# V of three token groups by wide products and SBUF-to-SBUF placing, with the zero fill, the w1 loads and the engine order rewritten around it

## The chip, the cores and the metric

The kernel runs on one core of a Trainium2 chip. TensorE multiplies matrices, VectorE (DVE in the profile) and GpSimd (POOL) work elementwise, ScalarE (ACT) evaluates functions, and SyncE (SP) issues nearly all transfers here. The metric is the device time in microseconds of one execution; four runs before the change have a median of 273.91 us (272.58 to 274.77).

## The reference

One block of a model: attention in a sliding window, then a token mixer, both with modulation by a condition vector `c`. S = 2048 tokens, D = 512, 32 heads of width 16, window 256, F = 1792.

```python
mod = (silu(c) @ w_mod).reshape(1, 6, 1, -1)          # sa, ca, ga, sb, cb, gb
h = layernorm(x) * (1 + ca) + sa
q, k, v = heads(h @ wqkv)
p = softmax(where(0 <= i - j < 256, q @ k.T / 4, -1e9))
x = x + ga * ((p @ v) @ wo)
h = layernorm(layernorm(x) * (1 + cb) + sb)
u = gelu(einsum('bsd,sf->bdf', h, w1) + b1)            # mixes tokens
x = x + gb * (einsum('bdf,fs->bds', u, w2) + b2).T
```

## The kernel before

**Stages.** The tokens are cut into four groups G of 512. For each group `proj` (line 518) normalizes x, transposes it to `h1T`, and forms Q, K and V; `attention` (line 854) is called for two units of 256 queries, and `post` (line 713) applies `wo`, adds the residual and makes the mixer's input `hb`. `partials` (line 787) and the loops at the end do the mixer's two large products: `pu<-hb,w1p` and `pu<-guT,w`.

**Attention.** It goes in 75 chunks. A chunk has scores for four heads at a time (`S`, TensorE, into `psa` and `psb`), two exponentials on ScalarE (`E` of 128x1536 and `F` of 128x512, into a ring of six `et` tiles), masks, and the product with V (`AV`, into `pxy`). In units 0 to 3 the masking is done on TensorE, by adding products of `edge_w` with `edge_n` or `edge_t`; in later units VectorE multiplies `et` by `maskt`. A unit's sums are normalized by `ln`, `rz` (ScalarE, tile `lz`) and `OT` (VectorE). Chunks 0 to 14 belong to group 0, 15 to 34 to group 1, 35 to 54 to group 2, 55 to 74 to group 3.

**V.** Keys go in blocks of 64. An AV product of a head pair has 128 rows: 64 keys of even heads above, 64 of odd heads below, and 32 weight columns, 16 for each parity; the half of V's columns that belongs to the other parity has to be zero. `VT` (line 244) is a ring of three such tiles, each filled with zeros once by `vt_zero` (line 512), all three on GpSimd. `v` (line 659) handles one block of 128 tokens: 32 matmuls of 128x32 weights with 256 columns put even heads into the upper partitions of `pv` and odd heads into the lower ones, so that two evacuations of 64 partitions each write straight to their places in `VT`. With four blocks in each of four groups there are 16 such blocks.

**K.** `k` (line 621) evacuates to `kb`, from which GpSimd (`kk`) writes two masked copies into `KT`.

**Order.** Every piece of work is an `Op` with dependencies. `ORDER` (line 42) is an order written out by hand number by number, with a letter where an operation isn't on its first engine; `run_order` (line 101) emits by it, and the emitted order is each engine's program order. The costs and positions in the `op` calls take no part in that. SP's queue also follows it: a transfer that waits holds up the ones behind it.

**w1.** `partials` frees the modulation weights' memory and then issues seven loads of 512 KB (`w1p`), which in the written order come together around chunk 18. A second half of each follows when the first has been used. The first product with w1 comes after chunk 46.

All instructions of the main part carry line 193, the wrapper that records order, so the profile is read by tile names.

## Time and profile before

| | |
|---|---|
| median of four runs | 273.91 us (272.58 to 274.77) |
| profiled execution: its time, its span | 273.24 us, 271.4 us |
| mean granted TensorE clock | 0.990 |
| TensorE busy | 250.9 us (92%) |
| VectorE busy | 209.0 us (77%) |
| ScalarE busy | 184.8 us (68%) |
| GpSimd busy | 68.3 us (25%) |
| HBM read, written | 22.03 MB, 2.10 MB |
| VT evacuations | 31 on VectorE, 686 ns each; 1 on ScalarE, 590 ns |
| VT zero fills on GpSimd | 3 of 3.51 us |

A group line of the profile names the engine and operation, written tile <- read tiles, the shape, the count, then busy time and mean duration in ns, then the idle time of the engine just before these instructions and what ended it. "issue" means that nothing shown was waited for. Busy time of TensorE counts pipelined matmuls by their modelled ends. In the timeline a line starts with start and length in us.

### The profile page before, as it was taken

What the parts mean: (1) busy time and instruction counts of PE and PEld (TensorE: products, weight loads), DVE (VectorE), ACT (ScalarE), POOL (GpSimd) and SP (SyncE); (2) the same over time, 40 slices, a digit from 0 to 9 for tenths busy, and PEclk for the clock granted to TensorE, in tenths of its full rate; (3) what the DMA queues carried; (4) which work ended last, traced back from release to release, by engine and by line L of the source; (5) the groups of instructions that cost most, each with busy time, mean ns of one, the idle gap of its engine ahead of it and who ended that gap; (6) DMA issues with size and microseconds to landing.
All of it is one profiled execution on the core that took longest, in us unless ns stands there. A gap on an engine that the chain in (4) does not pass through costs nothing.

```text
span 271.4 us, 10569 instructions
## 1 busy us (share of the span) xinstructions
PE 250.9 (92%) x4737; PEld 137.9 (51%) x4737; DVE 209.0 (77%) x442; ACT 184.8 (68%) x277; POOL 68.3 (25%) x131
## 2 busy tenths in 40 slices
PE   8879979699998999777999999999999999999993
PEld 2556647256766664445464454445544444444441
DVE  4788899578987678999977799999999751134685
ACT  3369969589998999999999999999632741000000
POOL 8994460135021844152102410140000000000000
PEclk9999999799999999999999999999999999999998
DMA  6998104940000000000020000095199800011121
GB/s 208 324 350 208 5 2 133 290 129 5 2 5 5 2 6 2 2 2 2 12 74 2 2 2 4 2 238 153 52 392 384 334 2 4 19 39 39 62 90 65
DMA packets 31445, 24.80 MB, mean 91 GB/s; under 512 B 6056, under 2 KB 29608, under 8 KB 31400
## 3 DMA queue, kind: packets, MB, share of 16 engines
q1 hardware_dynamic: 31392, 24.13, 29.4%
q8 instruction: 37, 0.61, 1.0%
q14 instruction: 8, 0.07, 0.1%
q10 hardware_dynamic: 8, 0.00, 0.0%
HBM read 22.03 MB, written 2.10 MB: 89 GB/s over the span
## 4 chain that ended last, share of the span: by engine, by line
PE 73%; ACT 11%; DVE 10%; issue 4%
PE pu L193 35%; PE pxy L193 13%; ACT et L193 10%; PE pq L193 8%; PE psa L193 8%; PE pa L193 4%; PE pv L193 3%; DVE st L193 2%; DVE VT L193 1%; DVE xn L193 1%; ACT lz L193 1%; PE pt L193 1%; DVE nm L193 1%; DVE et L193 1%; PE ps_b L193 1%
## 5 line engine op out<-in xcount | busy, mean ns | idle before, releaser
L193 ACT ACTIVATE et<-psa 128x1536 bf16<-128x1536 f32 x75 | 109.0, 1454 | 9.9 <-PE psb L193 7.2
L193 PE MATMUL pu<-hb,w1p 128*128 128x512 bf16 x224 | 53.0, 380 | 0.1
L193 PE MATMUL pu<-guT,w 128*128 128x512 bf16 x224 | 49.2, 379 | 0.0
L193 ACT ACTIVATE et<-psb 128x512 bf16<-128x512 f32 x75 | 44.6, 598 | 0.0
L193 POOL TENSOR_SCALAR KT<-kb,mask_par 128x512 bf16<-128x512 bf16 (+1 forms) x36 | 23.2, 652 | 63.1 <-DVE kb L193 63.1
L193 PE MATMUL pxy<-et,VT 128*32 128x192 bf16 (+3 forms) x960 | 37.5, 234 | 0.7 <-DVE OT L193 0.5
L193 PE MATMUL pxy<-et,ones_bd 128*32 128x192 bf16 (+3 forms) x960 | 37.6, 233 | 0.2 <-issue 0.2
L193 PE MATMUL pq<-h1T,wqkv 128*128 128x512 bf16 (+1 forms) x160 | 35.3, 347 | 2.6 <-DVE kb L193 1.5
L193 PEld LDWEIGHTS <-w 128*128 128x128 bf16 x224 | 21.9, 98 | 26.4
L193 PE MATMUL psa<-QT,KT 32*128 32x192 bf16 (+3 forms) x720 | 30.0, 230 | 5.1 <-ACT et L193 4.2
L193 PEld LDWEIGHTS <-w1p 128*128 128x128 bf16 x224 | 20.2, 98 | 24.9 <-issue 1.9
L193 PE MATMUL psb<-QT,KT 32*128 32x192 bf16 (+3 forms) x240 | 29.5, 231 | 2.7 <-issue 2.5
L193 PEld LDWEIGHTS <-KT 32*128 32x128 bf16 x960 | 15.6, 92 | 28.8 <-issue 27.2
L193 DVE SCALAR_TENSOR_TENSOR o<-pu,b2FM,bc_gb 128x512 f32<-128x512 f32 x16 | 12.0, 748 | 23.1 <-PE pu L193 23.0
L193 PEld LDWEIGHTS <-VT 128*32 128x32 bf16 x960 | 23.6, 97 | 7.7 <-issue 6.2
L193 DVE TENSOR_TENSOR et<-et,maskt 128x512 bf16<-128x512 bf16 (+2 forms) x56 | 23.8, 459 | 1.5 <-ACT et L193 1.4
L193 PEld LDWEIGHTS <-ones_bd 128*32 128x32 bf16 x960 | 23.2, 97 | 0.4 <-issue 0.3
L193 DVE CAST VT<-pv 64x512 bf16<-64x512 f32 x31 | 21.1, 686 | 2.9 <-PE pv L193 2.6
L193 DVE BATCH_NORM_STATS2 st<-x 128x6 f32<-128x512 bf16 x32 | 21.9, 683 | 1.9 <-DMA x<-in_A_x_dram 1.8
L193 PEld LDWEIGHTS <-wqkv 128*128 128x128 bf16 x160 | 13.4, 99 | 14.9 <-issue 5.4
L193 PE MATMUL pv<-wqkv,h1T 128*32 128x256 bf16 x512 | 17.8, 274 | 0.7 <-DVE h1T L193 0.6
L193 DVE CAST QT<-pq 128x512 bf16<-128x512 f32 (+1 forms) x19 | 13.1, 687 | 5.6 <-PE pq L193 5.5
(91 smaller groups left out, 347.4 us busy)
## 6 DMA issues: line engine op xcount, KB each, us to landing
w1p<-in_B_w_dram SPq DMA_DIRECT2D x14, 512.0 KB, 7.4
w<-in_B_w_dram SPq DMA_DIRECT2D x14, 512.0 KB, 8.9
wmod<-in_w_mod_dram SPq DMA_DIRECT2D x6, 512.0 KB, 6.6
x<-in_A_x_dram SPq DMA_DIRECT2D x16, 128.0 KB, 5.7
out_dram<-otile SPq DMA_DIRECT2D x16, 128.0 KB, 1.7
wqkv<-in_A_wqkv_dram SPq DMA_DIRECT2D x2, 384.0 KB, 6.1
wqkv<-in_A_wqkv_dram SPq DMA_DIRECT2D x1, 512.0 KB, 5.8
wod<-in_A_wo_dram SPq DMA_DIRECT2D x1, 512.0 KB, 9.5
```

What stands on the lines that cost most here:

```text
L193: ins = call(*args, **kwargs)
```

## The change

`v` now handles groups 1 to 3 only; group 0 keeps the old form as `v_first`. The new `v` takes 128 tokens as weights and all 512 V columns as moving data: four matmuls of 128x512. One evacuation writes the tile `vn`, parity by parity, with two buffers. Then four transfers of 64 partitions by 512 bytes, issued by SP, copy each parity's part of each 64-key block to its rows in `VT`. `VT` is laid out with the 16 heads of a parity innermost, so an AV weight tile reads 32 columns at a step of 16 elements; both evacuations therefore read PSUM at a step.

Around it: each zero fill is cut into four, of which five of twelve are put on VectorE and seven on GpSimd. The negated mean `nm`, where VectorE makes it, is computed as -2m + m by an operation of two tensors. Edges and masks are two operations; scores of units 0 to 3 wait for the edges, later masks for the masks. Each first-half w1 load waits for a `touch`, a two-element GpSimd copy from `et` of chunk 17, 20, ... 35, and the written order issues these loads one at a time between chunks 31 and 55. The order is new throughout; among the 1414 operations some change engine (for instance three Q evacuations on ScalarE instead of one, 13 normalizations `n2` on VectorE instead of 10).

```diff
@@ -43,58 +43,60 @@
 ORDER = """
-47 3 0 4 34 1 51 2 38 7 35 8 39 5 82 56 40 81 6 46 9 57 54 83 10 45 11 49 58 12 84 48 13 43 14 59 37 15 60 16 52 61
-85D 17 63 90D 18 55 91D 19 64 20 94 53 21 96D 97 44 95D 22 99A 50 86 78P 41 23 98A 106 36 24 109 25 107 42 26 108D
...
+45 3 0 4 41 78D 1 50 55 2 32 7 40 8 48 5 93 56 34 80P 6 37 9 57 52 10 58 90 42 11 46 12 79D 35 13 94 39 14 47 15 59
+95 96D 16 60 31 61 17 101D 63 18 62 102D 19 51 20 64 105 21 108 106A 33 22 110D 36 107A 38 109D 23 43 97 117 24 120
+121 25 118 122D 53 26 119A 49 123D 27 132 85D 28 133 140 29 134D 84P 141 196 98 30 142A 135 197 136 151 137D 152
...
 """
@@ -114,6 +116,7 @@
 E_BUFS = 6
+VN_BUFS = 2
 WARM = 24
@@ -241,7 +244,7 @@
     KT = [[kvpool.tile([P, 8, 2, KB], BF, name=f"KT{r}_{g}") for g in range(ND)] for r in range(3)]
-    VT = [kvpool.tile([P, 8, DH, 2 * DH], BF, name=f"VT{r}") for r in range(3)]
+    VT = [kvpool.tile([P, 8, 2 * DH, DH], BF, name=f"VT{r}") for r in range(3)]
     epool = att.enter_context(tc.tile_pool(name="epool", bufs=E_BUFS))
@@ -288,10 +291,6 @@
     def emit_masks():
-        if ADDED:
-            emit_edges()
-        if len(ADDED) == NU:
-            return
         tmpm = modw.tile([P, 2, 2, KB], BF, name="tmpm")
@@ -465,8 +464,12 @@
             mv, _, nm = box[box_key]
-            (ve if e == "DVE" else po).tensor_scalar(
-                out=nm[:, a:b], in0=mv[:, a:b, 0], scalar1=-1.0, scalar2=0.0, op0=ALU.mult, op1=ALU.add)
+            if e == "DVE":
+                ve.scalar_tensor_tensor(
+                    out=nm[:, a:b], in0=mv[:, a:b, 0], scalar=-2.0, in1=mv[:, a:b, 0], op0=ALU.mult, op1=ALU.add)
+            else:
+                po.tensor_scalar(
+                    out=nm[:, a:b], in0=mv[:, a:b, 0], scalar1=-1.0, scalar2=0.0, op0=ALU.mult, op1=ALU.add)
@@ -492,7 +495,7 @@
                     if pool:
-                        both.append(op(f"{tag}nm", {"DVE": 0.1, "POOL": 0.2}, lambda e, a=a, b=b: e_nm(e, a, b), deps=st_ops[:], pos=poss[i]))
+                        both.append(op(f"{tag}nm", {"DVE": 0.16, "POOL": 0.2}, lambda e, a=a, b=b: e_nm(e, a, b), deps=st_ops[:], pos=poss[i]))
                     for k in range(a, b):
@@ -509,8 +512,9 @@
-    vt_zero = [op("vz", {"DVE": 1.7, "POOL": 4.3}, lambda e, r=r: (ve if e == "DVE" else po).memset(VT[r][:], 0.0), pos=-20.0 + 5 * r)
-               for r in range(3)]
+    v_placed = []
+    vt_zero = [[op("vz", {"DVE": 0.45, "POOL": 0.95}, lambda e, r=r, n=n: (ve if e == "DVE" else po).memset(VT[r][:, 2 * n : 2 * n + 2, :, :], 0.0),
+                   pos=-20.0 + 5 * r, sh=True) for n in range(4)] for r in range(3)]
     k_done, q_done, v_done = {}, {}, {}
@@ -649,7 +653,7 @@
                 done = [
-                    op("kk", {"POOL": 0.1 + 0.6 * share}, lambda e, par=par: split(e, box["kb", g8], par), deps=[b, o_mp] + war, pos=pos, sh=True)
+                    op("kk", {"POOL": 0.1 + 0.66 * share}, lambda e, par=par: split(e, box["kb", g8], par), deps=[b, o_mp] + war, pos=pos, sh=True)
                     for par in range(2)
@@ -657,6 +661,41 @@
         def v(tb, pos):
+            halves = []
+            for i in range(2):
+                def e_v(e, i=i):
+                    if i == 0:
+                        box["v", tb] = ps_d.tile([P, D], F32, name="pv", tag="psd")
+                    for dc in (2 * i, 2 * i + 1):
+                        te.matmul(
+                            box["v", tb][:], lhsT=h1T[:, dc, tb * P : (tb + 1) * P], rhs=wqkv[:, dc, 2 * D : 3 * D],
+                            start=(dc == 0), stop=(dc == ND - 1),
+                        )
+
+                halves.append(op("v", {"PE": 0.427}, e_v, deps=[h_of[0, dc] for dc in range(2 * i + 2)] + halves + [o_w[2, 0]], pos=pos, cls="D", alloc=None if i else "psd"))
+
+            def e_ve(e):
+                box["vn", tb] = kvpool.tile([P, 2, DH, DH], BF, name="vn", tag="vn", bufs=VN_BUFS)
+                copy(e, box["vn", tb][:], box["v", tb][:].rearrange("p (a two d) -> p two d a", two=2, d=DH))
+
+            b = op("ve", {"ACT": 0.495, "DVE": 0.6}, e_ve, deps=[halves[1]] + (v_placed[-VN_BUFS] if len(v_placed) >= VN_BUFS else []), pos=pos)
+            halves[0].frees = [b]
+            mms.append(halves[1])
+            war = [av_ops[2 * G - 4, g] for g in range(ND)] if G >= 3 else [vt_zero[r3][tb]]
+            placed = []
+            for i in range(2):
+                for par in range(2):
+                    def e_vp(e, i=i, par=par):
+                        sp.dma_start(
+                            out=VT[r3][KB * par : KB * (par + 1), 2 * tb + i, DH * par : DH * (par + 1), :],
+                            in_=box["vn", tb][KB * i : KB * (i + 1), par, :, :],
+                        )
+
+                    placed.append(op("vp", {"SP": 0.4}, e_vp, deps=[b] + war, pos=pos, nbytes=64 * KBT))
+            v_placed.append(placed)
+            v_done[G, tb] = placed
+
+        def v_first(tb, pos):
             wv = wqkv[:, :, 2 * D : 3 * D].rearrange("p j (a two d) -> p j two a d", two=2, d=DH)
@@ -677,10 +716,10 @@
                 rows = slice(KB * par, KB * (par + 1))
-                copy(e, VT[r3][rows, 2 * tb : 2 * tb + 2, :, par * DH : (par + 1) * DH],
-                     box["v", tb][rows, :, :].rearrange("p i (a d) -> p i a d", d=DH))
-
-            war = [av_ops[2 * G - 4, g] for g in range(ND)] if G >= 3 else [vt_zero[r3]]
+                copy(e, VT[r3][rows, 2 * tb : 2 * tb + 2, par * DH : (par + 1) * DH, :],
+                     box["v", tb][rows, :, :].rearrange("p i (a d) -> p i d a", d=DH))
+
+            war = [av_ops[2 * G - 4, g] for g in range(ND)] if G >= 3 else [vt_zero[r3][tb]]
             bs = [op("ve", {"ACT": 0.53, "DVE": 0.62}, lambda e, par=par: e_ve(e, par), deps=[halves[1]] + war, pos=pos)
@@ -695,7 +734,7 @@
                         for tb in (2 * pn, 2 * pn + 1):
-                            v(tb, at + 0.5 + 0.3 * tb)
+                            v_first(tb, at + 0.5 + 0.3 * tb)
         else:
@@ -774,8 +813,12 @@
+    def touch_w1(pair, chunk):
+        t = w1t[pair, 0] = box["w1"].tile([P, 8, 2 * P], BF, name=f"w1p{pair}", tag=f"w1p{pair}")
+        po.tensor_copy(out=t[:, 0, 0:2], in_=et_of[chunk][:, 3, 0:2])
+
     def load_w1(pair, half):
-        t = box["w1"].tile([P, 8, 2 * P], BF, name=f"w1p{pair}", tag=f"w1p{pair}")
+        t = w1t[pair, 0] if half == 0 else box["w1"].tile([P, 8, 2 * P], BF, name=f"w1p{pair}", tag=f"w1p{pair}")
         sp.dma_start(out=t[:], in_=w1_v[:, 8 * half : 8 * half + 8, 2 * P * pair : 2 * P * (pair + 1)])
@@ -785,9 +828,9 @@
     def partials():
-        freed = op("w1free", {"SP": 0.0}, e_w1, deps=mod_ops + warm_ops + [o_fm, masks_built], pos=start_of(1) + 2.0)
         for pair in range(NF // 2):
-            w1_ops[pair, 0] = op("w1", {"SP": 0.4}, lambda e, pair=pair: load_w1(pair, 0), deps=[freed], pos=start_of(1) + 2.0, nbytes=512 * KBT)
+            chunk = touch_at[pair]
+            w1_ops[pair, 0] = op("w1", {"SP": 0.4}, lambda e, pair=pair: load_w1(pair, 0), deps=[touched[chunk]], pos=chunk + 0.5, nbytes=512 * KBT)
         p_of = {}
@@ -847,7 +890,8 @@
     avs = []
-    masks_built = op("masks", {"POOL": 6.0}, lambda e: emit_masks(), pos=-9.0)
+    edges_built = op("edges", {"POOL": 7.6}, lambda e: emit_edges(), pos=-9.0 if 0 in ADDED else 5.0)
+    masks_built = op("masks", {"POOL": 2.8}, lambda e: emit_masks(), pos=20.0 if 0 in ADDED else -9.0, sh=True)
@@ -933,7 +977,7 @@
             e_war = et_free[i - E_BUFS] if i >= E_BUFS else []
-            s = op(f"S{i}", {"PE": cost}, e_s2, deps=[o for g in gs for o in k_done[u, g] + q_done[u, g]] + ea_ops[-1:] + eb_ops[-2:-1] + [masks_built],
+            s = op(f"S{i}", {"PE": cost}, e_s2, deps=[o for g in gs for o in k_done[u, g] + q_done[u, g]] + ea_ops[-1:] + eb_ops[-2:-1] + ([edges_built] if added else []),
                    pos=i - 1.0, cls="S")
@@ -976,7 +1020,7 @@
                                     unit["xy"][32 * j : 32 * j + 32, 0 if isv else 1, KB * q0 : KB * (q0 + n)],
-                                    lhsT=VT[r][:, kbi, 4 * g8 + j, :] if isv else ones_bd[:],
+                                    lhsT=VT[r][:, kbi, :, 4 * g8 + j] if isv else ones_bd[:],
                                     rhs=et[:, j, KB * at : KB * (at + n)],
@@ -992,8 +1036,14 @@
                     last_mult.append(mult_ops[u, g8])
+            if i in touch_at:
+                touched[i] = op("touch", {"POOL": 0.15}, lambda e, i=i: touch_w1(touch_at.index(i), i), deps=[freed, xb], pos=i + 0.5)
+                parts.append(touched[i])
             et_free.append(parts)
...
+    touch_at = [start_of(1) + 2 + 3 * pair for pair in range(NF // 2)]
+    touched = {}
+    freed = op("w1free", {"SP": 0.0}, e_w1, deps=mod_ops + warm_ops + [o_fm, masks_built, edges_built], pos=start_of(1) + 2.0)
     last_mult = []
...
     et_free = []

```

## Prediction

> **What bounds the kernel now.** I read the busy slices first, then stage windows, then the chain of waits and the timeline where the chain leaves TensorE. The page's totals and slices (one digit is 6.8 us):
>
> ```profile
> PE 250.9 (92%) x4737; PEld 137.9 (51%) x4737; DVE 209.0 (77%) x442; ACT 184.8 (68%) x277; POOL 68.3 (25%) x131
> PE   8879979699998999777999999999999999999993
> DVE  4788899578987678999977799999999751134685
> ACT  3369969589998999999999999999632741000000
> PEclk9999999799999999999999999999999999999998
> ```
>
> TensorE is the end: nearly full from slice 20 on. Earlier it shows dents where another engine decides. The stage windows size these:
>
> ```profile
> 50.00:60.00 10.00, 8.52 (x176) 4.55 (x176) 5.14 (x10) 6.39 (x10) 1.89 (x3) 0.83 0.85 211
> 110.00:130.00 20.00, 15.47 (x488) 10.09 (x484) 19.51 (x48) 19.85 (x28) 7.20 (x9) 1.00 0.02 3
> 130.00:196.00 66.00, 65.43 (x1324) 33.39 (x1317) 58.20 (x135) 62.29 (x95) 9.68 (x12) 1.00 0.20 52
> 196.00:267.10 71.10, 71.02 (x330) 31.99 (x327) 42.18 (x73) 12.99 (x24) 0.00 (x0) 1.00 0.36 134
> ```
>
> Columns after the stretch: PE, PEld, DVE, ACT, POOL busy, granted clock, DMA share, GB/s. From 196 us TensorE is alone and full, so that stretch can only move, not shrink. Between 60 and 130 ScalarE is nearly full too; VectorE is full at 110 to 130, where TensorE idles 4.5 us. Before 60 us ScalarE still has holes. So gains come from stalls before 60 us, and from VectorE at 110 to 130.
>
> Two kinds of stall stand out in the timeline. First VectorE against GpSimd's zero fill of the V ring:
>
> ```profile
> 12.17 3.51 POOL L193 MEMSET VT<- 128x4096 bf16 x1
> 13.17 2.53 DVE L193 TENSOR_SCALAR nm<-mv 128x2 f32<-128x2 f32 x1
> 34.14 3.51 POOL L193 MEMSET VT<- 128x4096 bf16 x1
> 34.36 3.44 DVE L193 TENSOR_SCALAR xn<-x,mv,rs 128x512 bf16<-128x512 bf16 x1
> ```
>
> The tiny nm normally takes 0.16 us and xn 0.40; both end exactly with the fill, and both are on the chain that ended last. Second, the seven w1 loads:
>
> ```profile
> 42.97 10.80 SPq L193 DMA_DIRECT2D w1p<-in_B_w_dram  x7
> 48.69 0.23 PE L193 MATMUL psa<-QT,KT 32*128 32x128 bf16 x3
> 51.48 0.26 PE L193 MATMUL psb<-QT,KT 32*128 32x128 bf16 x1 [2.55 <-issue]
> 51.91 3.06 PE L193 MATMUL pq<-h1T,wqkv 128*128 128x512 bf16 x8
> 51.99 1.45 ACT L193 ACTIVATE et<-psa 128x1536 bf16<-128x1536 f32 x1 [2.72 <-PE psb L193]
> ```
>
> TensorE stops inside a group of four matmuls, waiting for nothing that is shown, while the loads fill the DMA engines; afterwards the clock is 0.50 from 51 to 54 us, and eight products take 3.06 us where they take 1.83 elsewhere.
>
> **The change part by part.** Durations are from the profiled execution, span 271.4 us, 273.24 us in all (1.84 around the span); the median shown is 273.91, 0.67 above it.
>
> **The V product** (12 blocks of groups 1 to 3; group 0 keeps the old form). These rows price old product, evacuation and the strided operand:
>
> ```profile
> L193 PE MATMUL pv<-wqkv,h1T 128*32 128x256 bf16 x512 | 17.8, 274 | 0.7 <-DVE h1T L193 0.6
> L193 DVE CAST VT<-pv 64x512 bf16<-64x512 f32 x31 | 21.1, 686 | 2.9 <-PE pv L193 2.6
> L193 PE MATMUL pxy<-et,VT 128*32 128x64 bf16 x240 | 8.2, 195 | 0.7 <-DVE OT L193 0.5
> L193 PEld LDWEIGHTS <-VT 128*32 128x32 bf16 x960 | 23.6, 97 | 7.7 <-issue 6.2
> ```
>
> A block of 32 narrow products takes 0.90 to 0.99 us in the chain; the four 128x512 products that replace it take 0.97, as the four q products do. TensorE gains 0, though it issues 56 instructions fewer per block.
>
> **Evacuation**: two casts of 0.69 become one of 128x512, 0.68 by the kb row. That frees 12 x 0.69 = 8.3 us of VectorE, but only where VectorE decides is it time. At 110 to 130 us six VT casts take 3.72 us of busy time; half, 1.9, goes. Behind it stand ScalarE (19.85 of 20) and the masks, so I count **-1.5**. The other six blocks fall where TensorE or ScalarE is full: 0. The new cast reads PSUM at a step of 32 elements, 16 in group 0's version; no row shows such a read. Bounds: 0, or double (0.5 us on about 20 casts, 10 us of VectorE, perhaps 4 of them exposed). Nearest row is the VT cast, which wrote in runs of 16 and was no slower than the contiguous kb; I take **+0.4**.
>
> **Placing**: 48 transfers of 32 KB on SP's queue. Issue: 0.43 to 1.06 us each in the x loads' rows (two in 0.86, eight in 8.49), so 1.7 to 4.2 per block; landing: 1.7 us for an output store, 4.0 for the quickest w1 load. The transfers follow the evacuation, so a V block is ready 3.4 to 8 us later than before. Attention consumes it two or more chunks later; 75 chunks in about 180 us are 2.4 us each, and six score buffers lie between. That is the cover for most blocks. In the written order the cover is thin once: group 1's third block has three of four transfers in SP's order behind those of group 2's second block, which wait for a later evacuation, and its first consumer, AV25, comes about one chunk after: up to 3 us late. What is queued behind AV25 on TensorE is S29 and so ScalarE's exponentials. With two vn buffers, the third block's evacuation waits on VectorE for the first block's landing; behind it there stand OT, x2 and the statistics, and the PSUM bank stays held. In the order this is 1 us in group 1, and little later. Bounds 0 and 8; I take **+1.5**.
>
> **Strided weights.** The 64-column AV groups follow each other every 0.03 us in the timeline, four at a time, so four loads of 32 weights are hidden in that. [...] A load of twice 0.03 would add 0.03 to each of 60 groups of 64 columns, 1.6 us, and nothing to the 128-, 192- and 256-column groups; four times would cost about 9 us. By the row alone 0; half of 1.6 would lie where TensorE is full, so I take **+0.4**. A gain is excluded: the same weights are loaded.
>
> **Zero fill.** Three fills of 3.51 become twelve, seven on GpSimd at about 0.9 and five on VectorE; nm on VectorE takes another instruction form. The first stall is worth 2.53 - 0.16 = 2.4; against it one VectorE fill (about 0.5) stands in the startup chain, and others stand before the x tiles arrive, where VectorE idled 1.75 us. The second is worth 3.44 - 0.40 = 3.0, but the ScalarE hole behind it is 1.96; next late there are the modulation broadcasts. I count **-1.5** and **-2.0**. Edges are now built before S0 and masks (2.7 us of small instructions) only around S7; S0 no longer waits for the masks' end at 12.1, which matters little as its K is ready at 12.3.
>
> **w1 loads.** The touches (seven tiny GpSimd copies, 0.2 us each by the edge copies' row, at most 1.4 together and hidden in GpSimd's 63 us of waiting for VectorE's kb) and the new order issue the seven loads one by one from chunk 31 to 55; in the order each still precedes its first product, which starts after chunk 46 as before. A touch waits for its chunk's exponential, and GpSimd's K masking queues behind it: touch 17 precedes masking that is needed at S20, a chunk or more away. Hole: 2.55, plus half of the 2.9 us at half clock, 1.45, makes 4.0. Another such hole, at 86.31 us with the DMA engines idle, is 0.66 long; that much I leave in. **-3.3**. [...] The row speaks for the loads: they are the only traffic, and the same 0.66 hole without traffic is four times shorter. I follow the row.
>
> **The new order.** Engine moves are small (a few norm steps between VectorE and GpSimd, two Q evacuations to ScalarE in the startup). The attention's lag behind the scores is unchanged within a chunk. Bounds -2 and +2, taken 0.
>
> Sum: -1.5 +0.4 +1.5 +0.4 -1.5 -2.0 -3.3 = -6.0. Span 265.4, execution 267.2, median **268.0 us**.
>
> **The rivals.** *The stalls move* (0.14): ScalarE, 98% busy from 60 to 110, absorbs VectorE's relief, and the startup gain dies at the next late thing. Speaking for it: ScalarE is 19.85 of 20 us at 110 to 130. Against: its holes before 60 are real, 1.96, 2.72 and 1.55. Then -3.3 from the loads, +2.3 of costs remain: -1.0, 272.9 us.
>
> *V comes late through SP's queue* (0.16), the slower side. Place: ten evacuations that wait for a vn buffer, and AV25. Price: evacuation 0.7 + issues 4.2 + landing 4.0 = 8.9 us between buffers, against a spacing of about 4.8 us between pairs of blocks in group 1; 4 us lost on two or three pairs, about 10 instead of 1.5: 276.5. It decides from a cost of 8.8 us on; with issue at 0.43 and landing at 1.7 (4.1 us in all) it doesn't. The 0.43 comes from lightly loaded moments, which these mostly are.
>
> *Strided weights dear* (0.05): the 9 us case, 276.6.
>
> *More is won* (0.07): all stalls go whole and V costs nothing: -2.4 -3.0 -4.0 -1.9 = -11.3, 262.6.
>
> **How the numbers follow.** My forecast holds 0.58 with its own range of 264.5 to 271.5. Within 0.5% of 273.91 (272.5 to 275.3, about what a measurement can tell from no change) lie 0.08 of the moved stalls' 0.14 and 0.02 of late V's 0.16; 0.06 of the moved stalls' ends below. Faster 0.58 + 0.07 + 0.06 = 0.71, same 0.10, slower 0.19. The range goes from 262.5 to 276.5.
>
> **What would show it.** Right: no nm or xn above 1.3 us; no PE hole above 1 us near the first w1 load and the clock at 1.00 after it; six VT casts fewer on VectorE at 110 to 130 in favour of three vn casts near 0.68; vp landing near 2 us; TensorE idling under 3.5 us at that stage. Wrong: vn casts above 1 us, AV groups of 64 columns spaced at 0.06, VectorE waiting for vp transfers, or PE waiting for DMA into VT.

## The result, and the profile after

| | before | after |
|---|---|---|
| median | 273.76 us (271.88 to 276.63, 49 runs) | 271.79 us (270.75 to 273.07, 30 runs) |
| profiled execution, its span | 273.24 us, 271.4 us | 271.92 us, 270.2 us |
| TensorE busy, idle in the span | 250.9 us, 20.5 us | 252.4 us, 17.8 us |
| VectorE busy | 209.0 us | 200.1 us |

The ratio is 0.9927, 95% interval 0.991 to 0.9944: faster by 2.0 us (1.5 to 2.5), a third of the 6.0 us that the sum had. Below, a ratio is made into microseconds with the 273.8 us of before. Each ratio is taken from the fast executions of a kernel and of the kernel before that ran beside it, whose medians went from 273.5 to 274.7 us, so a difference of ratios can be 0.9 us off the difference of the medians that are given; where that matters, both stand.

The page of the changed kernel, its totals and slices:

```profile
PE 252.4 (93%) x4401; PEld 135.9 (50%) x4401; DVE 200.1 (74%) x431; ACT 186.8 (69%) x278; POOL 67.6 (25%) x145
PE   7789999999998997889999999999998999999993
DVE  6778888757857859999676689899898750182594
ACT  3288999999998999999989999998711950000000
PEclk9999999999999999999999999999999999999999
```

TensorE's dents between 34 and 54 us and the dip of its clock are gone. In their place the first slices are a little lower, and the slice from 203 to 209 us, where TensorE had been full, has a dent. The stage windows (columns as in the prediction) size it:

```profile
50.00:60.00 10.00, 9.83 (x246) 5.27 (x238) 5.88 (x15) 9.32 (x14) 2.40 (x6) 1.00 0.11 25
110.00:130.00 20.00, 17.55 (x372) 9.04 (x368) 19.27 (x46) 18.88 (x27) 8.46 (x9) 1.00 0.31 80
130.00:196.00 66.00, 65.91 (x1286) 33.80 (x1283) 54.88 (x127) 61.35 (x92) 10.31 (x13) 1.00 0.24 59
196.00:267.10 71.10, 68.51 (x316) 30.65 (x314) 42.85 (x73) 12.39 (x23) 0.00 (x0) 1.00 0.39 139
```

Both stages that were expected to gain did: 50 to 60 us went from 8.52 to 9.83 busy at full clock, 110 to 130 from 15.47 to 17.55. But 196 to the end, full before (71.02 of 71.10), now idles 2.6 us, partly because the kernel ends earlier, partly for waits that are shown below. The stalls of VectorE behind the zero fill are gone; the timeline, as before start and length in us, with the fills as the change places them:

```profile
6.37 0.19 DVE L196 SCALAR_TENSOR_TENSOR nm<-mv 128x2 f32<-128x2 f32 x1
10.46 0.95 POOL L196 MEMSET VT<- 128x1024 bf16 x1
31.97 0.95 POOL L196 MEMSET VT<- 128x1024 bf16 x1
32.35 0.72 DVE L196 TENSOR_SCALAR xn<-x,mv,rs 128x512 bf16<-128x512 bf16 x1
```

The groups of the V work, for comparison with the four rows of the prediction:

```profile
L196 PE MATMUL pv<-wqkv,h1T 128*128 128x512 bf16 x48 | 12.9, 382 | 0.8 <-DVE kb L196 0.5 <-DVE h1T L196 0.3
L196 DVE CAST vn<-pv 128x512 bf16<-128x512 f32 x12 | 8.3, 690 | 7.5 <-DMA VT<-vn 3.4 <-PE pv L196 2.5 <-PE pxy L196 1.5
L196 PE MATMUL pxy<-et,VT 128*32 128x64 bf16 x240 | 10.0, 221 | 1.7 <-DVE OT L196 1.5
L196 PEld LDWEIGHTS <-VT 128*32 128x32 bf16 x960 | 33.1, 138 | 12.9 <-issue 10.3 <-DMA VT<-vn 1.0
```

The strided cast costs what a contiguous one costs (690 ns against 681 of `kb`); a load of V weights went from 97 to 138 ns, and the 64-column products behind it from 195 to 221. Two waits are new: the cast for an earlier transfer, and TensorE's load for one into `VT`. In the timeline:

```profile
59.70 0.69 DVE L196 CAST vn<-pv 128x512 bf16<-128x512 f32 x1 [2.33 <-DMA VT<-vn]
84.27 0.34 PE L196 MATMUL pxy<-et,VT 128*32 128x256 bf16 x4 [0.72 <-DMA VT<-vn]
```

The first is the third cast of group 1, the one that waits for the first block's landing. The second is a product of chunk 27 or 28. The first place was named in the prediction; the second lies two or three chunks behind the AV25 that it named.

How far the attention has come shows best where time goes. Start of the first exponential of a chunk, in us, from the timelines (e13, e16 and e17 are experiments below):

| chunk | before | after | e13 | e16 | e17 |
|---|---|---|---|---|---|
| 12 | 47.0 | 46.2 | 45.2 | 45.7 | 45.2 |
| 15 | 57.7 | 52.6 | 52.0 | 52.1 | 53.9 |
| 33 | 99.0 | 94.5 | 93.5 | 93.7 | 95.6 |
| 54 | 144.6 | 143.1 | 139.7 | 142.1 | 143.8 |
| 74 | 189.8 | 190.5 | 185.7 | 189.3 | 190.9 |
| span's end | 271.4 | 270.2 | 267.2 | 269.0 | 270.6 |

At chunk 15 the change is 5.1 us ahead of before, against the 6.8 us that its two kinds of stall were forecast to pay; by chunk 74 it is behind, of which some is only that more of the mixer's products lie before that chunk (what follows it takes 79.7 us instead of 81.6). At the end 1.2 us are left in these two executions.

### The profile page after: what moved, and what is told of

Same layout as the page of the kernel before. It is cut to its first block, busy times and chain, and to the rows that moved or that the text cites. A ratio compares the mean times of both kernels' runs of the same rounds, so it can differ in the third digit from the quotient of the medians.

```text
span 270.2 us, 10002 instructions
## 1 busy us (share of the span) xinstructions
PE 252.4 (93%) x4401; PEld 135.9 (50%) x4401; DVE 200.1 (74%) x431; ACT 186.8 (69%) x278; POOL 67.6 (25%) x145
## 4 chain that ended last, share of the span: by engine, by line
PE 64%; DVE 11%; ACT 8%; DMA 8%; SPq 5%; issue 1%; DVEq 0%; ACTq 0%
PE pu L196 33%; PE pxy L196 12%; PE psa L196 7%; ACT et L196 6%; PE pq L196 6%; SPq L196 5%; DMA VT<-vn 4%; DVE st L196 2%; DMA wqkv<-in_A_wqkv_dram 2%; PE pa L196 2%; PE pv L196 2%; DVE vn L196 2%; DMA wmod<-in_w_mod_dram 2%; ACT lz L196 2%; DVE part L196 1%
## 5 line engine op out<-in xcount | busy, mean ns | idle before, releaser
L196 PE MATMUL pu<-hb,w1p 128*128 128x512 bf16 x224 | 54.5, 380 | 1.3 <-DMA w1p<-in_B_w_dram 0.9
L196 PE MATMUL pxy<-et,VT 128*32 128x192 bf16 (+3 forms) x960 | 41.4, 249 | 2.9 <-DVE OT L196 1.8
L196 ACT ACTIVATE et<-psb 128x512 bf16<-128x512 f32 x75 | 44.0, 593 | 0.0
L196 PE MATMUL pxy<-et,ones_bd 128*32 128x192 bf16 (+3 forms) x960 | 40.1, 233 | 0.0
L196 PEld LDWEIGHTS <-VT 128*32 128x32 bf16 x960 | 33.1, 138 | 12.9 <-issue 10.3
L196 POOL TENSOR_SCALAR KT<-kb,mask_par 128x512 bf16<-128x512 bf16 (+1 forms) x36 | 22.6, 640 | 45.9 <-DVE kb L196 45.7
L196 PEld LDWEIGHTS <-ones_bd 128*32 128x32 bf16 x960 | 27.3, 105 | 0.0
L196 DVE TENSOR_TENSOR et<-et,maskt 128x512 bf16<-128x512 bf16 (+2 forms) x56 | 24.5, 469 | 0.6 <-ACT et L196 0.5
L196 DVE TENSOR_TENSOR OT<-pxy,lz 128x256 bf16<-128x256 f32 x32 | 13.4, 419 | 9.2 <-ACT lz L196 8.8
L196 PE MATMUL pv<-wqkv,h1T 128*32 128x256 bf16 (+1 forms) x176 | 17.1, 303 | 0.9 <-DVE kb L196 0.5
L196 PE MATMUL pa<-wod,OT 128*128 128x512 bf16 x64 | 17.0, 381 | 0.1
```

The costliest lines, as they stand in the source:

```text
L196: ins = call(*args, **kwargs)
```

## The experiments

Theories at the start: (A) the parts pay what the sum says, and something new takes some 4 us back; candidates are the strided weights, the transfers and the new order; (B) the parts pay less, because stalls only move. "Old order" means the written order of the kernel before.

### Parts alone, in the old order

**The w1 loads (e5).** Each load follows a two-element GpSimd copy from the newest `et`; in the order the loads stand at chunks 30, 32, 35, 38, 41, 44 and 49.

```diff
         t = box["w1"].tile([P, 8, 2 * P], BF, name=f"w1p{pair}", tag=f"w1p{pair}")
+        if half == 0:
+            po.tensor_copy(out=t[:, 0, 0:2], in_=et_of[max(et_of)][:, 3, 0:2])
```

> The kernel before, its own order, with the seven first w1 loads taken apart: each is issued behind a two-element GpSimd copy from the newest score tile, at chunks 30, 32, 35, 38, 41, 44 and 49. Theory A (the burst costs what the prediction counted): no hole of 2.5 us at 49 us, clock 1.00 there, 2.5 to 4 us faster, 0.985 to 0.991. Theory B (the time won there is given back later, at a stage that another engine sets): hole gone, but within 1 us, 0.996 to 1.003.

270.87 us, 0.9907 (0.9878 to 0.9937): 2.5 us. The window of the stage, in this kernel:

```profile
50.00:60.00 10.00, 9.65 (x295) 6.10 (x294) 8.37 (x18) 9.50 (x14) 3.80 (x7) 1.00 0.02 5
```

TensorE is busy for 9.65 us instead of 8.52, at full clock. The hole goes with the seven loads together, as the row said: it is gone here, where TensorE's instructions are the same, and in e4 (below), which leaves the loads together, it is there: 2.3 us of idle TensorE before `psb`, put to "issue". What in the burst held TensorE up no run shows. The sum had 3.3.

The lowered clock is less firmly tied to the loads. In e4's profiled execution the hole is there and the clock stays at 1.00; e6 (below) has a lowered clock already before its loads (0.57 on the mean from 38 to 42 us); one execution of e5 has 0.990 and took 272.12 us. Of 91 executions of the kernel before that ran beside the experiments, 17 have a mean granted clock of 0.996 or more and a median of 272.3 us, the other 74 a median of 273.9. All 30 of the change have 0.996 or more. So some 1.6 us of a gain over the kernel before can be clock alone: at 0.996 and above the change stands at 271.8 against 272.3, half a microsecond ahead. What lowers the clock stays open.

**The zero fills.** First cut into four pieces, moved behind the scores of chunks 8 and 13, and `nm` as an operation of two tensors (e6); then that with the loads of e5 (e7).

```diff
-(ve if e == "DVE" else po).memset(VT[r][:], 0.0)
+[(ve if e == "DVE" else po).memset(VT[r][:, 2 * n : 2 * n + 2, :, :], 0.0) for n in range(4)]
```

> The kernel before, its own order, with each zero fill in four pieces, the fills of the second and third V tile moved to stretches where GpSimd waits (around chunks 8 and 13), and nm on VectorE as an operation of two tensors. Theory A: no nm or xn above 1.4 us, 2.5 to 4 us faster, 0.985 to 0.991. Theory B (given back later): within 1 us, 0.996 to 1.003.

272.76 us, 0.9972 (0.9942 to 1.0002).

> The kernel before with both: w1 loads taken apart and fills cut and moved. Theory A (both gains stand and add): 5 to 7.5 us faster, 0.972 to 0.982, and better than the changed kernel. Theory B: at most 2 us, 0.992 to 1.000.

270.75 us, 0.9907 (0.9872 to 0.9942), the same as e5. The timeline of e7 shows why:

```profile
34.23 3.63 POOL L203 MEMSET VT<- 128x1024 bf16 x4
34.46 3.54 DVE L203 TENSOR_SCALAR xn<-x,mv,rs 128x512 bf16<-128x512 bf16 x1
```

Four pieces back to back hold the normalization for 3.54 us as one fill had held it for 3.44. So these two runs did not take the second stall away, and say nothing of its price. The first one they did: `nm`, now of two tensors, takes at most 0.208 us in e6 and 0.164 in e7. By e7 against e5 that is worth nothing, give or take 1.3 us, where the sum had 1.5. In e12 the second and third tile are zeroed by transfers from a tile of zeros; with the loads of e5 and `nm` of two tensors:

```diff
+        if r == 0:
+            po.memset(VT[r][:], 0.0)
+        else:
+            for n in range(8):
+                sp.dma_start(out=VT[r][:, n, :, :].rearrange("p a c -> p (a c)"), in_=zt[:])
```

> The kernel before in its own order with the w1 loads taken apart, the second and third V tile zeroed by transfers from a zero tile instead of by GpSimd, and nm on VectorE as an operation of two tensors; the fill of the first tile stays on GpSimd. The same without these edits of the fills ran at 0.991. Theory A (the two stalls of VectorE are worth the 3.5 us counted): nm and xn near 0.16 and 0.40 us, 0.976 to 0.981. Theory B (what waits behind them is late anyway): stalls gone, 0.987 to 0.992.

268.78 us, 0.9817 (0.9788 to 0.9846), and no `xn` on VectorE above 0.785 us, no `nm` there above 0.223. Against e5 that is 2.5 us for both stalls, give or take 1.1 (2.1 by the medians); the sum had 3.5. The first V tile is still filled in one piece, and `nm` runs in the middle of that fill:

```profile
12.21 3.51 POOL L203 MEMSET VT<- 128x4096 bf16 x1
13.20 0.16 DVE L203 SCALAR_TENSOR_TENSOR nm<-mv 128x2 f32<-128x2 f32 x1
```

In the kernel before, the same fill held `nm` for 2.53 us. So the first stall went by the form of `nm`, not by anything done to the fill.

**Strided weights (e4).** V stays as it is in the kernel before, but is read as weights at a step of 16 elements, so that heads are mixed up in the output.

```diff
-lhsT=VT[r][:, kbi, 4 * g8 + j, :]
+lhsT=VT[r][:, kbi, :, :].rearrange("p a c -> p (a c)").rearrange("p (c a) -> p c a", a=DH)[:, :, 4 * g8 + j]
```

> The kernel before with the V weights read at a step of 16 elements from its own layout (wrong heads; only the time counts). Theory A (strided read costs TensorE): loads at 138 ns, 2 to 3.5 us slower than before, 1.007 to 1.013. Theory B (covered): within 0.8 us, 0.997 to 1.003.

275.44 us, 1.008 (1.0045 to 1.0115): 2.2 us slower, with the loads at 138 ns as in the change.

**The V change (e10).** On top of e5: wide products, one evacuation, four transfers, strided weights; fills as before. The first of a block's two old evacuations becomes the new one, the second the four transfers.

```diff
 def e_v(e, i=i):
+    if G:
+        ...
+        for dc in (2 * i, 2 * i + 1):
+            te.matmul(
+                box["v", tb][:], lhsT=h1T[:, dc, tb * P : (tb + 1) * P], rhs=wqkv[:, dc, 2 * D : 3 * D],
+                start=(dc == 0), stop=(dc == ND - 1),
+            )
+        return
```

> The kernel before in its own order with the w1 loads taken apart, and V of groups 1 to 3 by the wide products, one evacuation and four transfers, strided layout: the V change without the new order. The same without the V change ran at 0.991. If the V change wins in itself (VectorE's relief larger than strided loads and transfers): 0.983 to 0.988. If it loses in an order that was not written for it: 0.991 to 0.998.

271.15 us, 0.9908 (0.9883 to 0.9933), the same as e5. In the old order the V change is worth nothing in sum, give or take 1 us.

### Parts taken out of the change

**e1** reads V's weights contiguously (elements of other heads); **e2** leaves out the 48 transfers (V of groups 1 to 3 stays zero); **e3** forms V the old way wholly, in the new order; **e8** has six `vn` buffers instead of two.

```diff
 e1
-lhsT=VT[r][:, kbi, :, 4 * g8 + j]
+lhsT=VT[r][:, kbi, :, :].rearrange("p c h -> p (c h)")[:, 32 * (4 * g8 + j) : 32 * (4 * g8 + j + 1)]
 e2
-sp.dma_start(out=VT[r3][...], in_=box["vn", tb][...])
+return
 e3
-copy(e, box["vn", tb][:], box["v", tb][:].rearrange("p (a two d) -> p two d a", two=2, d=DH))
+for par in range(2):
+    rows = slice(KB * par, KB * (par + 1))
+    copy(e, VT[r3][rows, 2 * tb : 2 * tb + 2, :, par * DH : (par + 1) * DH],
+         box["v", tb][rows, :, :].rearrange("p i (a d) -> p i a d", d=DH))
 e8
-VN_BUFS = 2
+VN_BUFS = 6
```

> The changed kernel, with the V weights of each AV product read as 32 contiguous elements instead of at a step of 16; it reads the same number of elements from the same tile, but the wrong heads, so only its time counts. Theory A (the strided weight read costs TensorE time: the V weight loads went from 97 to 138 ns and a block of 64 AV matmuls from 1.22 to 1.33 us, 30 blocks): loads back at 97 ns, blocks at 1.22 us, 2.5 to 3.5 us faster than the changed kernel, ratio to the kernel before 0.980 to 0.984. Theory B (the attention stage is set by ScalarE and by waits, the slower loads are covered): blocks at 1.22 us but the time within 0.8 us of the changed kernel, 0.990 to 0.994.

268.54 us, 0.9824 (0.9786 to 0.9862): 2.8 us faster than the change. The group of V loads in e1:

```profile
L196 PEld LDWEIGHTS <-VT 128*32 128x32 bf16 x960 | 23.9, 96 | 14.1 <-issue 10.9
```

It is back at 96 ns. The stride costs 2.2 to 2.8 us (e4, e1), where the sum had 0.4.

> The changed kernel without the 48 placing transfers, so V of groups 1 to 3 is left at zero and only the time counts. Theory A (the transfers' issue and landing delay the third and later evacuations on VectorE and the first AV products of a group; DMA and SP hold 13% of the chain): 2 to 4 us faster than the changed kernel, 0.978 to 0.986. Theory B (the transfers are covered by the order, and the chain only names what happened to come last): within 0.8 us of it, 0.990 to 0.994.

269.88 us, 0.9876 (0.9842 to 0.9911): 1.4 us faster than the change.

> The changed kernel with six vn buffers instead of two. If the transfers cost by VectorE's wait for a vn buffer (3.4 us in two waits): those waits gone, 0.7 to 1.5 us faster than the changed kernel, 0.987 to 0.990. If they cost by SP's order and the AV products' waits: within 0.5 us, 0.991 to 0.994.

271.07 us, 0.9908 (0.9876 to 0.994): 0.5 us less than the change, within the interval, though VectorE no longer waits for a transfer in its trace. So the buffers alone are not the price.

> The changed kernel's order, fills, touches and w1 loads, with V made wholly the old way: narrow products, two evacuations of 64 partitions straight into the old layout, no transfers. Theory A (the V change itself loses, strided weights and transfers together costing more than twelve saved evacuations): 2 to 5 us faster than the changed kernel, 0.975 to 0.986. Theory B (the V change is what wins, by VectorE's 8.3 us): 1.5 to 4 us slower than the changed kernel, 0.998 to 1.007.

272.37 us, 0.997 (0.994 to 0.9999): the V change is worth 1.2 us in the new order, on the edge of what these intervals can tell. With the stride at 2.8 and the transfers at 1.4 there, its product and evacuation would have to be worth 5.4, so the terms are not the same in both orders.

### The order

None of this explained where 4 us went: loads 2.5, fills 2.5 and V 0 make 5.0, and the change has 2.0. **e13** is the old order with the parts in it: the edit of e10 (and so of e5), the fills of e12, `nm` of two tensors. It does not have the change's engine moves, its edges and masks apart, its many small fills and its chunks for the touches; "new order" below stands for all of these but the fills, and no run takes them apart.

> The kernel before with its own order, and into it all that the change brings beside the order: w1 loads one by one, wide V product, one evacuation, four transfers, V with heads innermost read at a stride, no second and third fill on GpSimd (transfers of zeros instead), nm as an operation of two tensors. The change as made stands at 0.993. Theory that the new order gives back what the parts win: this one is clearly faster than the change, 0.979 to 0.986 (270.87 us with the loads alone, less 2 for the fills, V at 0), some 2 to 4 us. Rival, the parts get in each other's way whatever the order: 0.990 to 0.994, as the change. It also shows whether the last w1 load is late here: if so, that is not the new order's.

268.89 us, 0.9796 (0.9755 to 0.9837): 5.6 us faster than before, and 3.6 faster than the change (give or take 1.2; 2.9 by the medians). Control **e16** is the change, in its order, with the fills of e13:

```diff
+    def fill(e, r, n):
+        if r == 0:
+            (ve if e == "DVE" else po).memset(VT[r][:, 2 * n : 2 * n + 2, :, :], 0.0)
+        else:
+            for m in (2 * n, 2 * n + 1):
+                sp.dma_start(out=VT[r][:, m, :, :].rearrange("p a c -> p (a c)"), in_=zt[:])
```

> The change with its own order; only the zero fills of the second and third V tile come by transfers early in SP's order, in place of eight small fills on VectorE and GpSimd. Theory that the order itself costs the 3 us: 0.989 to 0.994, at most 1 us better than the change (0.993), since the small fills no longer stall anything. Rival, the small fills cost it: 0.980 to 0.985, as the parts in the old order (0.980).

271.16 us, 0.9895 (0.9859 to 0.9931). The many small fills are not the bulk of it: with equal fills the new order is 2.7 us slower than the old, give or take 1.5 (2.3 by the medians, and no execution of one reaches into the other's). Where? Windows of the change, then of e13 (columns as before):

```profile
60.00:85.00 25.00, 23.16 (x656) 14.84 (x656) 17.86 (x39) 24.05 (x36) 11.51 (x17) 1.00 0.09 20
196.00:215.00 19.00, 17.70 (x82) 7.83 (x81) 16.81 (x34) 7.63 (x16) 0.00 (x0) 1.00 0.99 358
```

```profile
60.00:85.00 25.00, 24.37 (x679) 15.16 (x680) 18.90 (x42) 24.50 (x37) 4.26 (x7) 1.00 0.10 23
196.00:215.00 19.00, 19.00 (x90) 8.62 (x89) 16.35 (x31) 9.93 (x18) 0.00 (x0) 1.00 0.92 349
```

TensorE idles 1.2 us more from 60 to 85 and 1.3 us more from 196 to 215; it idles 1.2 more before 13 us too. At the chunk marks little of this shows at first, 52.1 us in e16 against 52.0 in e13 at chunk 15 and 93.7 against 93.5 at chunk 33, but these show the attention alone: up to chunk 33 TensorE has idled 6.7 us in e16 and 4.5 in e13, so other work has been put off. **e17** asks for the startup: all that the old order has before the scores of chunk 15 in that order (in the numbers of the change), the rest in the new one, fills as in e16.

```diff
-45 3 0 4 41 78D 1 50 55 2 32 7 40 8 48 5 93 56 34 80P 6 37 9 57 52 10 58 90 42 11 46 12 79D 35 13 94 39 14 47 15 59
+47 3 0 4 34 1 51 2 38 7 35 8 39 5 93 56 40 90 91 6 46 9
+57 54 94 10 45 11 49 58 12 95 48 13 43 14 59 37 15 60 16 52 61 96D
...
```

> As e16, but everything up to the scores of chunk 15 (groups 0's attention and group 1's projection) is emitted in the old order, the rest in the new one. If the new order loses in the startup: 0.980 to 0.985, as all parts in the old order (0.980). If it loses later (idle TensorE at 60 to 110 us and after 196 us): 0.988 to 0.993. By the idle times of TensorE 1.2 us of 3.4 are lost before 13 us, 0.6 from 30 to 60, 1.3 from 60 to 110 and 1.3 after 196, so some 0.985 to 0.989 is likeliest.

272.22 us, 0.9936 (0.9911 to 0.9961). It gains nothing. In the table above e17 has e13's lead at chunk 12 (45.2), is 1.7 us behind e16 at chunk 15, past the seam, and from chunk 15 on takes as long as e16 (216.7 us against 216.9; e13 takes 215.2). The seam is the experiment's own, so of the startup it says only that an old one does not rescue the new rest.

**The wait after 196 us (e15).** In the change TensorE waits at 203.76 us for a second-half w1 load, which stands in SP's order behind three w2 loads. e15 moves that one load ahead of them.

```diff
-1183 1118 1158 1160 1195 1011 1184 1019 1012 1186 1161 1020 1140
+1183 1118 1140 1158 1160 1195 1011 1184 1019 1012 1186 1161 1020
```

> The change as it is, with one w1 load moved: the last second-half load, which stands in SP's order behind three w2 loads that wait for attention's memory, goes ahead of them. If the two waits near 204 and 206 us (0.93 and 0.37 us) are time: 270.5 us, 0.988, and TensorE idles 1 us less after 196. If the end is set by something else there: 271.8 us, 0.993.

270.92 us, 0.9871 (0.9833 to 0.9908). The timelines, of the change and then of e15:

```profile
203.76 1.96 PE L196 MATMUL pu<-hb,w1p 128*128 128x512 bf16 x8 [0.93 <-DMA w1p<-in_B_w_dram]
206.08 2.10 PE L196 MATMUL pu<-hb,w1p 128*128 128x512 bf16 x9 [0.37 <-DVE part L196]
```

```profile
202.21 1.96 PE L207 MATMUL pu<-hb,w1p 128*128 128x512 bf16 x8 [0.93 <-DVE part L207]
204.54 3.83 PE L207 MATMUL pu<-hb,w1p 128*128 128x512 bf16 x17 [0.37 <-DVE part L207]
```

The load now stands in SP's queue with the five before it, ahead of all w2 loads, and the waits stayed, to the hundredth, under the name of VectorE's `part`; e1, where no load was moved, has them under that name too. So the load was not what TensorE waited for. The two waits go with the new order: the change, e1, e2, e3, e8, e9, e15, e16 and e17 all have them, 0.93 or 0.94 and 0.37 us long, and no kernel in the old order idles TensorE more than 0.11 us from 196 to 215. What differs is the place of VectorE's `part`, in the change and then in e13:

```profile
196.20 0.68 DVE L196 TENSOR_TENSOR part<-pu,part 128x512 f32<-128x512 f32 x1
200.97 0.68 DVE L196 TENSOR_TENSOR part<-pu,part 128x512 f32<-128x512 f32 x1
```

```profile
193.56 0.66 DVE L203 TENSOR_TENSOR part<-pu,part 128x512 f32<-128x512 f32 x1
196.22 0.69 DVE L203 TENSOR_TENSOR part<-pu,part 128x512 f32<-128x512 f32 x1
```

In the change VectorE works without a gap through nine steps of the last normalizations between one `part` and the next, 4.1 us; in e13 it is 2.0 us at most there. That this makes the wait is a reading of the traces; no run moved these steps. The lead of e15 over the change is there long before (143.1 against 141.9 us at chunk 54), where nothing was altered, so it is not the moved load's; this run leaves it unexplained, and a difference of 0.9 us between two kernels here should be read with that in mind.

**Transfers in the old order (e18).** The same removal as e2, made in e13 (V of groups 1 to 3 stays zero).

> All parts in the old order (0.980), without the 48 placing transfers; V of groups 1 to 3 stays zero. In the new order leaving them out gained 1.4 us (0.993 to 0.988). Theory that the new order makes their price: in the old one neither VectorE nor TensorE waits for a placing transfer in the trace, so 0.977 to 0.982, no gain. Rival, the transfers cost by themselves (SP's queue, traffic in the memory): 0.973 to 0.976, some 1.4 us less here too.

268.67 us, 0.9801 (0.9763 to 0.9839), e13's ratio. In the old order leaving the transfers out gains nothing, give or take 1.6 us (0.2 by the medians), and the waits of e13's VectorE casts show no transfer at all:

```profile
DVE vn L203 <- PE pv L203: 4.3, 4, 2.2
```

Those of the change (total us, times, longest) do:

```profile
DVE vn L196 <- DMA VT<-vn: 3.4, 2, 2.3
DVE vn L196 <- PE pv L196: 2.5, 3, 1.6
DVE vn L196 <- PE pxy L196: 1.5, 1, 1.5
```

So the 1.4 us of e2 (give or take 1.1; 1.9 by the medians) are most likely the price of where the transfers stand, not of the transfers. They are not the whole loss: without any transfer the orders still differ, e2 and e18 by 2.0 us (1.2 by the medians), and e3 and e12, which both form V the old way but have different fills, by 4.2 (3.6 by the medians).

### A faster kernel

As the stride is the dearest of the costs that the V change adds (2.2 to 2.8 us by e4 and e1, against 0 to 1.4 for the transfers by e18 and e2), V can keep its old layout. The evacuation writes each head into its place of a `vn` tile whose other places were zeroed once, and the transfers copy 1 KB per partition, zeros included; then the second and third V tile need no fill. **e9** is that in the new order, **e11** on top of e5 in the old, **e14** is e11 with `nm` of two tensors and `vn` zeroed by six transfers.

```diff
-copy(e, box["vn", tb][:], box["v", tb][:].rearrange("p (a two d) -> p two d a", two=2, d=DH))
+copy(e, box["vn", tb][:].rearrange("p (t x d) -> p t x d", t=2, d=DH)[:, :, 0 : 2 * DH : 2, :],
+     box["v", tb][:].rearrange("p (a two d) -> p two a d", two=2, d=DH))
...
-in_=box["vn", tb][KB * i : KB * (i + 1), par, :, :],
+in_=box["vn", tb][KB * i : KB * (i + 1), 2 * DH * DH * par : 2 * DH * DH * (par + 1)],
```

> The changed kernel with the old V layout (32 contiguous columns per head pair). The evacuation writes each parity's 16 columns between zeros into one of three fixed vn tiles that are zeroed once, and the transfers carry 1 KB per partition, zeros included; only the first V tile is still zero-filled. Theory A (strided weights are the largest cost of the V change): V weight loads at 97 ns, 2 to 4 us faster than the changed kernel, 0.978 to 0.985, and better than both kernels. Theory B (transfers of 64 KB are dearer than strided loads): 0.989 to 0.996.

269.13 us, 0.9828 (0.9795 to 0.986): 2.7 us faster than the change, in the change's own order. Beside the stride, eight small fills went and three came.

> The same with the padded vn tiles and the contiguous layout; the fills of the second and third V tile fall away, three vn tiles of 2 KB per partition are zeroed instead. If strided weights cost 2 to 3 us here too, that much faster than the one with the strided layout. 0.976 to 0.986; 0.988 to 0.993 if the old order hides it.

267.70 us, 0.978 (0.9756 to 0.9805).

> The fastest so far (old order, loads one by one, wide V product, V contiguous through zero-padded vn tiles, 0.978), with nm as an operation of two tensors and the zeros of the vn tiles brought by six transfers instead of GpSimd fills. If the stall behind the remaining fill still costs: 0.5 to 2 us less, 0.971 to 0.977. If it was already gone or is covered: 0.976 to 0.980.

265.84 us, 0.9683 (0.9646 to 0.9719): 8.7 us faster than before, the fastest of all. The edit against e11:

```diff
-for t in vnt:
-    eng.memset(t[:], 0.0)
+for t in vnt:
+    for n in range(2):
+        sp.dma_start(out=t[:, D * n : D * (n + 1)], in_=zt[:])
```

Its groups of V work:

```profile
L203 PEld LDWEIGHTS <-VT 128*32 128x32 bf16 x960 | 23.3, 96 | 10.5 <-issue 9.1
L203 DVE CAST vn<-pv 128x512 bf16<-128x512 f32 x12 | 8.3, 688 | 3.7 <-PE pv L203 3.6
```

Against e13 it differs in V's layout, with the transfers and zero fills that go with it, and gains 3.1 us (0.9683 against 0.9796), give or take 1.5: in line with the stride's price, but not of the stride alone.

## Why the prediction was wrong

The direction was right, though by little where the clock is equal (0.5 us, under e5), and the two kinds of stall were the right places; the size was wrong by a factor of three. Term by term, with what the runs put in its place:

| step | forecast | measured, us |
|---|---|---|
| V product, evacuation and its strided read | -1.1 | about -2.2 in the old order, worked out, with 2 us either way: e10 equals e5 although the stride costs 2.2 (e4) and the transfers 0 (e18) |
| placing transfers | +1.5 | 1.4 in the new order (e2), 0 in the old (e18) |
| strided weights | +0.4 | 2.8 (e1), 2.2 (e4) |
| zero fills | -3.5 | -2.5 (e12 against e5); of this about 0 for the first stall (e7 against e5) |
| w1 loads | -3.3 | -2.5 (e5), a part of it clock |
| all of these, old order | -6.0 | -5.6 together (e13) |
| the new order | 0 | +3.6 (change against e13, its small fills included), +2.7 with equal fills (e16 against e13) |

**The step that failed is "The new order", bounds -2 and +2, taken 0.** The parts together pay what the sum said, within 0.4 us; the reordering gave back half or more of it, 2.7 to 3.6 us (2.3 to 2.9 by the medians), where the bound was 2. That bound had been drawn from engine moves and the attention's lag within a chunk, without asking what the order does over a whole stage. What the runs show of the loss: leaving out the transfers gains 1.4 us in the new order and nothing in the old (e2, e18), and the change's trace has waits for them where that of e13 has none. The trace also has 1.2 us more idle TensorE before 13 us, 1.2 us at 60 to 85 us, and 1.3 us at 203 to 206 us, where `pu` waits for VectorE's `part`; the second overlaps with the transfers in part (0.72 us of `pxy` behind `VT` at 84 us), the third is in every kernel of the new order and in none of the old. That the wait for `part` costs its 1.3 us was not shown: e15 moved a load and left the wait standing. Which entries of the order make the loss is open.

**Strided weights.** The second error, 2 us, and hidden in the sum, since other terms missed the other way. The row of 97 ns is of a contiguous read and says nothing of a stride: no run shows the +0.4, nor the doubled load it was estimated from, and the runs showed 138 ns a load and 2.2 to 2.8 us (e4, e1) in their place. The estimate, 1.6 us for a load twice as long (60 groups at 0.03 are 1.8), went into the sum as 0.4: half of it "would lie where TensorE is full", and that was halved again towards the row's 0. From 130 to 196 us TensorE was busy for 65.43 of 66.00 us in the kernel before, which left 0.57 us to hide an added TensorE cost in, so that half should have counted whole; measured was more than the whole 1.6. The load grew to 1.4 times its length and not to twice, but on all 960 loads, and the wider products slowed too (128 columns from 220 to 235 ns, 192 from 247 to 252, 256 from 275 to 289), for which the prediction had nothing. Which of the machine's limits makes 138 ns no run here tells.

**Strided PSUM read.** Forecast +0.4 between 0 and 4; measured 690 ns against 681 contiguous, nothing.

**Transfers.** The late places were nearly those named: the third cast of group 1 waited 2.33 us, a product 0.72, two or three chunks behind AV25. SP's issue took 461, 594 and 1731 ns (least, median, most), landing 1.8, 2.7 and 6.1 us. That +1.5 is close to e2's 1.4 is in part luck, as the old order shows no such cost; the rival of 10 us did not happen.

**Fills and loads.** Both mechanisms held, each some 0.8 to 1 us smaller than summed. Of the fills it was the first stall that paid nothing (e7), though 1.5 was counted; it ended by the form of `nm`. Of the loads the hole ended with the burst, but the lowered clock, counted with 1.45, is not in every execution of the kernel before.

**The rivals.** "The stalls move" gave 272.9, the nearest to the measured 271.8, but hardly by its mechanism: in the old order the removal of the stalls pays 5.0 us of the 6.8 (e5, e12), and only for the first stall, which paid nothing in e7, does it fit. "Strided weights dear" named a cost that was there at 2.8 and not 9. "More is won" needed that no new cost arises. The case that happened, a new order that costs 3 us, was in no rival, although the diff rewrites every line of it.

**Signs.** Of those listed as right nearly all came: no `nm` or `xn` on VectorE above 0.85, no hole at the loads, clock at 1.00, casts at 0.69 (four at 110 to 130 instead of three), TensorE idle 2.45 there; the transfers landed in 2.7 us instead of near 2. Of those listed as wrong two came as well: VectorE waiting for the placing transfers, and TensorE waiting for a transfer into `VT`.

## What to carry to other kernels

When a change rewrites a hand-written order together with the work, the order is the largest unknown in the sum (here 2.7 to 3.6 us, where the bound was 2): give it its own bounds, as wide as the gains, and test it by putting the new work into the old order. Count an added cost on the engine that sets the end in full where that engine is full: here the strided weights, taken at 0.4, cost 2.2 to 2.8 us (e4, e1). And ask what a cleverer layout for an evacuation costs its reader: here 960 weight loads of 138 ns instead of 97 paid for 12 casts, and padding the evacuation's tile with zeros got the same placing with loads of 96 ns (e14).

## What the runs showed of the hardware

A weight load of 128x32 bf16 read at a step of 32 bytes took 138 ns instead of 97 (96 when read contiguously again, in e1), and the contiguous `ones_bd` loads between them 105 instead of 97. Four GpSimd fills of 0.9 us back to back held a VectorE operation for 3.54 us in e7, where one fill had held it for 3.44: cutting the fill up did nothing there, while single pieces of 0.95 us in the change left no VectorE `nm` or `xn` above 0.85. A tiny VectorE operation of two tensors took 0.16 us in the middle of a 3.51 us fill (e12) that had held its one-tensor form for 2.53. A VectorE cast reading PSUM at a step of 32 elements was as fast as a contiguous one (690 ns against 681). The granted clock was 0.50 from 51 to 54 us in the profiled execution of the kernel before, but not in all its executions: those with a mean of 0.996 or more have a median of 272.3 us, the others 273.9. And a wait's name in the trace need not be its cause: the same gap of 0.93 us was put to a load in one kernel and to VectorE in the next.
